# Block attention and a top-1 mixture of experts on one core: one cast and one subtraction for eight transposed blocks

## The chip, the cores and the metric

The kernel runs on one core of a Trainium2 chip. The metric is device time in microseconds, from the start of one execution to its end; less is better. Engines are named as the profile names them: PE (TensorE matmuls and transposes), PEld (its weight loads), DVE (VectorE), ACT (ScalarE), POOL (GpSimd) and SP, which only issues DMAs here.

## The reference, cut to what matters

Eight batches of eight heads, 576 positions, 64 numbers each. Attention is masked by blocks of 64: a query sees the keys of its own block and of all blocks before it. The outputs of all heads, 4608 rows of 512, then go through a mixture of eight experts, of which each row uses the one with the highest gate.

```
scores = (q @ k.T) / 8;  scores = -1e9 where block(query) < block(key)
attn   = exp(scores - rowmax);  attn /= sum(attn);  x = attn @ v
expert = argmax(x @ w_gate)
y      = relu(x @ w1[expert]) @ w2[expert] * gate(x) * sigmoid(x @ w_output_gate)
```

## The kernel before

Attention is worked on in 32 **pairs** of heads of one batch. A pair passes through the engines as a pipeline: `round_of(g)` writes the work of step g, four steps to a pair, and each step holds pieces of several pairs at different ages. Here a **period** is four steps (r = 0, 1, 2, 3), in which one pair enters and one leaves. The order on PE, ACT and DVE is the order in which the code is written; all three run it strictly in that order, and wait on semaphores of other engines. SP issues the loads (`fetch`, `fetch_v`) some steps ahead.

What a pair goes through, with the names that matter below:

- `turn` (r = 3): PE transposes eight 128 x 128 blocks of k and q, which lie in the tile `nat`, into one PSUM tile `ps_s`. Each number is kept as the sum of two 16-bit ones: ACT casts the transposed block to 16 bits (tile `tr0`, the high part), DVE subtracts it from the PSUM value (tile `tr1`, the low part). `turn_blocks` does this for four blocks at a time, and is called twice. The two tiles show as `tr` in the rows.
- The **ninth block** holds the 64 first positions of k and q, which fit in no block of 128. It is transposed in the next step r = 0, in `turn_max`, into the tile there.
- `max_tile` 0, 1 and 2 (r = 0, 1, 2): products of the high parts alone, of which DVE takes the row maxima (`nmx`). The maxima of the last query tile against the odd first 64 keys come apart, by `odds_rest` and `max_rest` (r = 3), in a corner of the tile of `prob_tile` 2; `nmr` holds them. Two small DVE operations (L199, L200) then finish the maxima as 16-bit numbers in `nmz`.
- `turn_max` (next r = 0): PE transposes `nmz`, and ACT copies the result to `qe`, by which the maxima are subtracted inside the products.
- `prob_tile` 3, 0, 1, 2 (r = 0, 1, 2, 3): the products in full, and their exponentials by ACT into `pcr` and `pc`.
- `lows` (POOL): the low part of each exponential, `lpc` and `lpcr`.
- `values` and `values_odd` (r = 2, 3): the products with v, into the PSUM tile `ps_v`; `norm` (DVE, r = 0) divides by the sums, and `turn_x` transposes the result for the gate.

`ps_s` has three buffers of two PSUM banks each, taken in turn; a period takes ten of them (and a few more where a batch ends). A tile that takes a buffer waits until the tile three places before it has been read by its last reader. Once in four periods a batch is complete, and `finish_batch` adds small pieces for its gates and for the table of rows.

After the attention come the experts (from about 600 us), whose products fill PE; no line of them is changed.

Of the kernel before, what the change touches and what calls it, by code (L numbers as in the profile page):

```python
# [8 lines left out]
F16 = mybir.dt.float16  # L9
BF16 = mybir.dt.bfloat16  # L10
F32 = mybir.dt.float32
I32 = mybir.dt.int32
U32 = mybir.dt.uint32
AF = mybir.ActivationFunctionType
ALU = mybir.AluOpType
AX = mybir.AxisListType
# [4 lines left out]
P = 128  # L21
# [5 lines left out]
def block_attention_top1_moe(  # L27
# [11 lines left out]
    nc = tc.nc  # L39
# [4 lines left out]
    NT = 5  # L44
# [4 lines left out]
    SCALE = D ** -0.5  # L49
# [19 lines left out]
    NPR = B * NP  # L69
# [5 lines left out]
    sb = tc.alloc_tile_pool(name="sb", bufs=2)  # L75
    small = tc.alloc_tile_pool(name="small", bufs=2)
# [5 lines left out]
    last_max, last_lo, last_exp = [None], [None], [None]  # L82
# [3 lines left out]
    def banks():  # L86
        return ps_s.tile([P, 2, 512], F32, name="ps_s")
# [4 lines left out]
    class Pair:  # L92
# [22 lines left out]
        def turn(self, ps=None):  # L115
            self.room()
            ps = banks() if ps is None else ps
            ps = ps.rearrange("p a (b n) -> p (a b) n", n=P)
            for w in range(2):
                self.turn_blocks(ps[:, 4 * w:4 * w + 4], 1 + 4 * w)  # L120

        def turn_blocks(self, ps, r, hi=None):
            n = ps.shape[1]
            for j in range(n):
                nc.tensor.transpose(ps[:, j], self.nat[:, r + j].rearrange("p h d -> p (h d)"), ident)  # L125
            th, tl = (self.tr[c][:, r:r + n] for c in range(2))
            (hi or nc.scalar.copy)(th, ps)  # L127
            nc.vector.tensor_tensor(tl, ps, th, ALU.subtract)  # L128

# [59 lines left out]
                    os[ab][:, c0:c0 + R0], self.asks(0, ab, n, n + 1)[:, 0], self.odd(0, ab, 0, R0), start=True, stop=True  # L189
                )  # L190

        def odds_rest(self, ps):
            self.odds([ps[:, ab] for ab in range(2)], 3, 256)

        def max_rest(self, ps):
            self.nmz = nmzs[self.p % 2]
            nmr = small.tile([P, 2], F32, name="nmr")
            last_max[0] = nc.vector.tensor_reduce(nmr, ps[:, :, 256:320], AX.X, ALU.max, negate=True)  # L198
            nc.vector.tensor_tensor(self.nmx[:, 3, :], self.nmx[:, 3, :], nmr, ALU.min)  # L199
            nc.vector.tensor_scalar(  # L200
                self.nmz.rearrange("p t (h c) -> p t h c", h=2)[:, :, :, 0], self.nmx, 1.0 / MS, None, ALU.mult
            )

        def turn_max(self):
            ps = banks()
            pm = ps[:, 0].bitcast(F16)
            for t in range(NT):
                nc.tensor.transpose(pm[:, P * t:P * t + P], self.nmz[:, t, :], ident16)
            self.qe = sb.tile([P, 640], F16, name="qe")
            nc.scalar.copy(self.qe, pm[:, 0:640])  # L210
            if self.p + 2 < NPR:
                pairs[self.p + 2].turn_blocks(ps[:, 1:2, 0:P], 0)

        def prob_tile(self, i, ps=None):
            names = ("pc13", "pc0", "pc2", "pcr")
            if i == 0:
                self.pt = [sb.tile([P, 2, n], F32, name=x) for x, n in zip(names, (512, 512, 256, S // 2))]
                self.pl = [sb.tile([P, 2, n], F16, name="l" + x) for j, (x, n) in enumerate(zip(names, (512, 512, 256, S // 2)))]
            ps = banks() if ps is None else ps
            qe = self.qe[:, 0:512].rearrange("p (n x) -> p n x", x=P)  # L220

            def products(os, ks, qs):
                half = [slice(64 * ab, 64 * ab + 64) for ab in range(2)]
                for j, (kc, qc) in enumerate(((0, 0), (1, 0), (0, 1), (2, 2))):
                    for ab in range(2):
                        nc.tensor.matmul(os[ab], ks(kc, ab), qs(qc, ab), start=j == 0, stop=j == 3)  # L226

            if i < 3:
                for c, c0 in (((1, 0), (3, 384)), ((0, 0),), ((2, 0),))[i]:
                    m = P * (4 - c)  # L230

                    def ks(kc, ab):
                        return self.keys(kc, ab, c, c + 1)[:, 0] if kc < 2 else kext[64 * ab:64 * ab + 64, c]

                    def qs(qc, ab):
                        return self.asks(qc, ab, c, 4) if qc < 2 else qe[64 * ab:64 * ab + 64, c:4]

                    products([ps[:, ab, c0:c0 + m].rearrange("p (n x) -> p n x", x=P) for ab in range(2)], ks, qs)
                ap = ps[:, :, 0:256] if i == 2 else ps
            else:  # L240
                flat = ps.rearrange("p a n -> p (a n)")

                def ks(kc, ab):
                    return self.odd(kc, ab, 0, R0) if kc < 2 else kext[64 * ab:64 * ab + 64, 4, 0:R0]

                def main(qc, ab):
                    return self.asks(qc, ab, 0, 4) if qc < 2 else qe[64 * ab:64 * ab + 64]

                def last(qc, ab):
                    return self.odd(qc, ab, R0, P) if qc < 2 else self.qe[64 * ab:64 * ab + 64, 576:640]  # L250

                halves = [flat[64 * ab:64 * ab + 64] for ab in range(2)]
                products([x[:, 0:512].rearrange("p (n x) -> p n x", x=P) for x in halves], ks, main)
                products([x[:, 512:S] for x in halves], ks, last)
                ap = flat[:, 0:S].rearrange("p (a n) -> p a n", a=2)
            self.ap = ap
            if i != 2:
                self.exps(i)

        def exps(self, i):  # L260
            last_exp[0] = nc.scalar.activation(self.pt[i], self.ap, AF.Exp, scale=SCALE)  # L261

        def lows(self, i):
            eng = nc.gpsimd if self.p < NPR - 4 else nc.vector
            eng.tensor_tensor(self.pl[i], self.pt[i], self.high(i), ALU.subtract)  # L265

        def high(self, j):
            return self.pt[j].bitcast(BF16)[:, :, 1::2]
# [53 lines left out]
        def turn_x(self):  # L322
            if self.hp == 0:
                xTs[self.b] = sb.tile([P, NP, S], F32, name="xT")
            pa = banks().rearrange("p a n -> p (a n)")
            for t in range(NT):
                nc.tensor.transpose(pa[:, P * t:P * t + P], self.xn[:, t], ident)
            xT = xTs[self.b]
            nc.scalar.copy(xT[:, self.hp, 0:512], pa[:, 0:512])
            nc.scalar.copy(xT[:, self.hp, 512:S], pa[:, 576:640])  # L330
            if self.hp == NP - 1:
                later.append(finish_batch(self.b, xT))

    xTs = {}

    with tc.high_priority(offset=3000):
        ident16 = const.tile([P, P], F16, name="ident16")
# [66 lines left out]
    def opening():  # L404


        x, y = Pair(0), Pair(1)
        x.fetch()
        y.fetch()
        rest = ps_v.tile([P, 2, 512], F32, name="ps_v")  # L410

        def turned(z):
            z.turn()
            z.turn_blocks(rest[:, z.p:z.p + 1, 0:P], 0, nc.vector.tensor_copy)

        turned(x)
        at(1, lambda: turned(y))
        return x, y

    with tc.manual_schedule(engines={mybir.EngineType.PE}), tc.high_priority(offset=2000):  # L420
        pairs = dict(enumerate(opening()))
# [49 lines left out]
    def pay_later():  # L471
        for g in list(later):
            if next(g, later) is later:
                later.remove(g)
# [534 lines left out]
    def round_of(g):  # L1009

        r = g % 4

        def do(back, name, *args):
            p, rr = divmod(g - back, 4)
            if 0 <= p < NPR:
                getattr(pairs[p], name)(*args)

        if r == 0:
            do(4, "turn_max")
            if g < 4 * NPR + 11:  # L1020
                do(16, "turn_x")
            do(12, "norm")
            do(0, "max_tile", 0)
            pay_later()
            do(8, "prob_tile", 3)
        elif r == 1:
            do(1, "max_tile", 1)
            do(5, "prob_tile", 0)
            do(9, "lows", 3)
            pay_later()  # L1030
            if g == 4 * NPR + 9:
                do(13, "turn_x")
        elif r == 2:
            do(6, "lows", 0)
            do(6, "prob_tile", 1)
            do(2, "max_tile", 2)
            pay_later()
            do(10, "values", 0)
            do(6, "lows", 1)
        else:  # L1040
            ps = banks() if g < 4 * NPR + 4 else None
            do(7, "prob_tile", 2, ps)
            do(3, "odds_rest", ps)
            do(3, "max_rest", ps)
            do(7, "exps", 2)
            do(-5, "turn")
            pay_later()
            do(11, "values_odd")
            do(11, "values", 1)
            do(7, "lows", 2)  # L1050
        for fn in events.get(g, ()):
            fn()
        pay_later()
# [124 lines left out]
```

## Time and profile before

| what | value |
| --- | --- |
| median of 3 runs (lowest, highest) | 980.36 us (976.35, 983.75) |
| the profiled execution: its time, its span | 985.71 us, 984.0 us |
| PE busy | 790.8 us, 80% of the span |
| PEld busy | 554.5 us, 56% |
| DVE busy | 608.7 us, 62% |
| ACT busy | 458.5 us, 47% |
| POOL busy | 395.9 us, 40% |

The busy shares are means over two stages. In the attention, which is about the first 560 us, PE is busy some seven tenths of the time and its granted clock lies between 0.7 and 0.9 of full speed; with the experts PE is busy nearly all the time at the full clock. The granted clock is a mean: the engine runs at 1.2 or at 2.4 GHz, and 0.5 in a stretch means that all of it was at 1.2. A row of a timeline tells the start, the duration and the work of an instruction (or of some alike), and in square brackets how long its engine had been idle before it and what ended that.

### The profile page before, as it was taken

The numbers are of one execution on the slowest core, as the hardware profiler recorded it, in microseconds if no ns is written. First come the engines' busy times: TensorE is split into PE (matmuls) and PEld (weight loads), VectorE is DVE, ScalarE is ACT, GpSimd is POOL, SyncE is SP. The second block draws the span as 40 slices with busy tenths as digits, with TensorE's granted clock in tenths as the row PEclk, the third lists the DMA queues.
The fourth block names the chain that finished last, engine by engine and source line by source line (L and its number), as shares of the span: only waits on it lengthen the run. The fifth ranks groups of instructions, "written<-read, shape, count | busy, mean of one in ns | idle before, by whom it ended". The sixth has DMA issues, their size and how long they took to land. (4 is left out here: it accounts for less than half of the span.)

```text
span 984.0 us, 23380 instructions
## 1 busy us (share of the span) xinstructions
PE 790.8 (80%) x9438; PEld 554.5 (56%) x9438; DVE 608.7 (62%) x962; ACT 458.5 (47%) x668; POOL 395.9 (40%) x348
## 2 busy tenths in 40 slices
PE   5676767767776767768676787799999999999995
PEld 3455545555554545555454574567766776667762
DVE  6555575656565665656668634778685968577560
ACT  2433434344343343343343521767665767475550
POOL 3544345455454363464425633634223233241101
PEclk9777797888798897888887799799999999999998
DMA  6342423224233323223125105897899998972330
GB/s 154 78 97 51 97 50 84 63 50 97 50 71 76 81 66 85 62 66 82 26 53 192 47 14 192 178 310 214 298 292 318 338 317 210 281 221 70 129 109 35
DMA packets 203748, 130.48 MB, mean 133 GB/s; under 512 B 157456, under 2 KB 175920, under 8 KB 203632
## 3 DMA queue, kind: packets, MB, share of 16 engines
q1 hardware_dynamic: 195584, 109.61, 40.8%
q0 software_dynamic: 8048, 19.29, 6.6%
q8 instruction: 76, 1.25, 0.6%
q14 instruction: 40, 0.33, 0.1%
HBM read 126.03 MB, written 19.34 MB: 148 GB/s over the span
## 5 line engine op out<-in xcount | busy, mean ns | idle before, releaser
L896 PEld LDWEIGHTS <-w1b 128*128 128x128 f16 (+1 forms) x2208 | 176.7, 98 | 25.2 <-issue 3.4
L896 PE MATMUL ps_s<-xt,w1b 128*128 128x256 f16 (+5 forms) x1920 | 175.8, 253 | 1.7 <-issue 1.3
L925 PE MATMUL ps_o<-w2b,hh 128*128 128x512 f16 (+1 forms) x560 | 168.6, 383 | 9.4 <-ACT hh L904 8.9
L125 PE MATMUL ps_s<-ident,nat 128*128 128x128 f32 x286 | 63.5, 341 | 135.5 <-DVE tr L128 104.9
L265 POOL TENSOR_TENSOR lpc<-pc 128x1024 f16<-128x1024 f32 (+1 forms) x84 | 133.8, 1612 | 54.5 <-ACT pc L261 54.1
L775 DVE TENSOR_TENSOR w2b<-w2f,w2b 128x1024 bf16<-128x1024 f32 x80 | 92.7, 1219 | 94.8 <-ACT w2b L773 82.5
L175 DVE TENSOR_REDUCE nmx<-ps_s 128x2 f32<-128x896 f32 (+4 forms) x160 | 120.1, 788 | 45.3 <-PE ps_s L188 24.4
L261 ACT ACTIVATE pc<-ps_s 128x1024 f32<-128x1024 f32 (+1 forms) x96 | 82.1, 880 | 119.4 <-DVE nmr L198 55.4
L128 DVE TENSOR_TENSOR tr<-ps_s,tr 128x512 f16<-128x512 f32 (+1 forms) x94 | 52.7, 561 | 134.7 <-ACT tr L127 132.7
L125 PEld LDWEIGHTS ps_s<-ident,nat 128*128 128x128 f32 x286 | 37.5, 163 | 154.4 <-DVE tr L128 113.1
L934 POOL DMA_INDIRECT out_dram<-ys,ids x38 | 49.4, 1300 | 153.2 <-ACT ys L933 90.9
L925 PE MATMUL ps_o<-w2b,hl 128*128 128x512 f16 x280 | 106.9, 382 | 0.0
L925 PEld LDWEIGHTS <-hh 128*128 128x128 f16 x560 | 54.8, 98 | 72.8 <-ACT hh L904 9.0
L226 PE MATMUL ps_s<-tr,tr 64*128 64x384 f16 (+5 forms) x768 | 95.6, 328 | 0.0
L127 ACT CAST tr<-ps_s 128x512 f16<-128x512 f32 (+1 forms) x94 | 45.3, 481 | 103.8 <-PE ps_s L125 103.8
L775 DVE TENSOR_TENSOR w1b<-w1f,w1b 128x1024 bf16<-128x1024 f32 x80 | 92.6, 1217 | 0.7 <-ACT w1b L773 0.6
L226 PEld LDWEIGHTS <-tr 64*128 64x128 f16 (+1 forms) x1152 | 56.2, 110 | 50.7 <-issue 31.7
L274 PE MATMUL ps_v<-vh,pc 128*128 128x65 f16 x640 | 82.8, 214 | 1.0 <-DVE xn L313 0.7
L265 POOL TENSOR_TENSOR lpcr<-pcr 128x576 f16<-128x576 f32 x28 | 32.1, 1146 | 127.6 <-ACT pcr L261 127.6
L275 PE MATMUL ps_v<-vl,pc 128*128 128x64 f16 x640 | 82.5, 212 | 0.5 <-issue 0.5
L276 PE MATMUL ps_v<-vh,lpc 128*128 128x65 f16 x640 | 82.4, 212 | 0.4 <-issue 0.4
L933 ACT ACTIVATE ys<-ps_o,ids 128x512 f32<-128x512 f32 (+1 forms) x38 | 26.1, 686 | 118.1 <-PE ps_o L925 100.0
(208 smaller groups left out, 1640.1 us busy)
## 6 DMA issues: line engine op xcount, KB each, us to landing
w1f<-in_moe_w_dram SPq DMA_DIRECT2D x80, 512.0 KB
w2f<-in_moe_w_dram SPq DMA_DIRECT2D x80, 512.0 KB
nat<-in_k_dram SPq DMA_DIRECT2D x64, 128.0 KB
nat<-in_q_dram SPq DMA_DIRECT2D x64, 128.0 KB
vn<-in_v_dram SPq DMA_DIRECT2D x64, 128.0 KB
x_d<-xn SPq DMA_DIRECT2D x32, 256.0 KB
hh<-in_moe_w_dram SPq DMA_DIRECT2D x4, 512.0 KB
hl<-in_moe_w_dram SPq DMA_DIRECT2D x4, 512.0 KB
```

The costliest lines, as they stand in the source:

```text
L125: nc.tensor.transpose(ps[:, j], self.nat[:, r + j].rearrange("p h d -> p (h d)"), ident)
L128: nc.vector.tensor_tensor(tl, ps, th, ALU.subtract)
L175: last_max[0] = nc.vector.tensor_reduce(self.nmx[:, t, :], ps[:, :, c0:c1], AX.X, ALU.max, negate=True)
L226: nc.tensor.matmul(os[ab], ks(kc, ab), qs(qc, ab), start=j == 0, stop=j == 3)
L261: last_exp[0] = nc.scalar.activation(self.pt[i], self.ap, AF.Exp, scale=SCALE)
L265: eng.tensor_tensor(self.pl[i], self.pt[i], self.high(i), ALU.subtract)
L274: nc.tensor.matmul(o, hi, self.vh[rows, j], start=first, stop=False)
L275: nc.tensor.matmul(o[:, 0:D], hi, self.vl[rows, j], start=False, stop=False)
L276: nc.tensor.matmul(o, lo, self.vh[rows, j], start=False, stop=last)
L775: eng.tensor_tensor(lo[at], src[at], hi[at], ALU.subtract)
L896: nc.tensor.matmul(ph[:, f4].rearrange("p (h n) -> p h n", n=w), wv[:, cc, f, :], xv[:, cc], start=(k == 0), stop=(k == 3 * KD - 1))
L925: nc.tensor.matmul(py, hv[:, f, h], wv[:, f, :], start=(k == 0), stop=(k == 3 * KF - 1))
```

## The change

- `turn` makes all eight transposes first, and then calls the new `halves` once: one cast and one subtraction of 128 x 1024 in the place of two of 128 x 512 each.
- The new `mixed` takes the place of `turn_max`, `odds_rest` and the first half of `max_rest`. In one PSUM tile at the start of r = 0 it has the transposes of the last pair's `nmz`, the ninth block of the pair to come, and the odd maxima's products of the pair now beginning. ACT copies `qe`; after `norm`, DVE takes the odd maxima and makes both halves of the ninth block (its cast was on ACT).
- The end of the maxima (the two small operations of `max_rest`) moves from r = 3 to r = 2, behind `max_tile` 2.
- `prob_tile` 2 takes its exponential at once, and shares its tile with nothing.
- `lows` 0 and 1 are cut into two instructions each, one for each head.

```diff
         def turn(self, ps=None):
...
-            for w in range(2):
-                self.turn_blocks(ps[:, 4 * w:4 * w + 4], 1 + 4 * w)
-
-        def turn_blocks(self, ps, r, hi=None):
-            n = ps.shape[1]
-            for j in range(n):
+            self.turn_blocks(ps, 1)
+            self.halves(ps, 1)
+
+        def turn_blocks(self, ps, r):
+            for j in range(ps.shape[1]):
                 nc.tensor.transpose(ps[:, j], self.nat[:, r + j].rearrange("p h d -> p (h d)"), ident)
-            th, tl = (self.tr[c][:, r:r + n] for c in range(2))
+
+        def halves(self, ps, r, hi=None):
+            th, tl = (self.tr[c][:, r:r + ps.shape[1]] for c in range(2))
             (hi or nc.scalar.copy)(th, ps)
             nc.vector.tensor_tensor(tl, ps, th, ALU.subtract)
...
         def lows(self, i):
             eng = nc.gpsimd if self.p < NPR - 4 else nc.vector
-            eng.tensor_tensor(self.pl[i], self.pt[i], self.high(i), ALU.subtract)
+            n = 2 if i < 2 else 1
+            for ab in range(n):
+                sl = slice(ab, ab + 1) if n == 2 else slice(0, 2)
+                eng.tensor_tensor(self.pl[i][:, sl], self.pt[i][:, sl], self.high(i)[:, sl], ALU.subtract)
...
+    def mixed(g):
+
+        p = g // 4
+        z, x, y = (pairs[j] if 0 <= j < NPR else None for j in (p - 1, p, p + 1))
+        y = y if p > 0 else None
+        ps = banks()
+        pm = ps[:, 0].bitcast(F16)
+        if z:
+            for t in range(NT):
+                nc.tensor.transpose(pm[:, P * t:P * t + P], z.nmz[:, t, :], ident16)
+        if y:
+            y.turn_blocks(ps[:, 1:2, 0:P], 0)
+        if x:
+            x.odds([ps[:, ab] for ab in range(2)], 3, 320)
+        if z:
+            z.qe = sb.tile([P, 640], F16, name="qe")
+            nc.scalar.copy(z.qe, pm[:, 0:640])
+        yield
+        if x:
+            x.nmr = small.tile([P, 2], F32, name="nmr")
+            last_max[0] = nc.vector.tensor_reduce(x.nmr, ps[:, :, 320:384], AX.X, ALU.max, negate=True)
+        if y:
+            y.halves(ps[:, 1:2, 0:P], 0, nc.vector.tensor_copy)
...
         if r == 0:
-            do(4, "turn_max")
+            parts = mixed(g) if g < 4 * NPR + 4 else iter(())
+            next(parts, None)
             if g < 4 * NPR + 11:
                 do(16, "turn_x")
             do(12, "norm")
+            next(parts, None)
             do(0, "max_tile", 0)
...
             do(2, "max_tile", 2)
+            do(2, "max_rest")
...
-            ps = banks() if g < 4 * NPR + 4 else None
-            do(7, "prob_tile", 2, ps)
-            do(3, "odds_rest", ps)
-            do(3, "max_rest", ps)
-            do(7, "exps", 2)
+            do(7, "prob_tile", 2)
             do(-5, "turn")
```

The order of PE in r = 3, around `turn`, first before and then changed. `nat` is the tile of loaded k and q, `ident` the identity matrix, and names in the brackets are semaphores: of DMA queues, of ACT (Activation) and of DVE.

```order
L188 LDWEIGHTS tr_2167
L188 MATMUL ps_s<-tr_2167 128x64
L125 MATMUL ps_s<-ident,nat 128x128 [waits DMAHW2_49,DMAHW1_49,Activation_49]
L125 MATMUL ps_s<-ident,nat 128x128 x3
L125 MATMUL ps_s<-ident,nat 128x128 [waits DMAHW7_49,DMAHW6_49,DVE_49]
L125 MATMUL ps_s<-ident,nat 128x128 x3
L274 LDWEIGHTS pcr
L274 MATMUL ps_v<-vh_101,pcr 128x65
```

```order
L212 LDWEIGHTS kext
L212 MATMUL ps_s<-qe,kext 128x256
L124 MATMUL ps_s<-ident,nat 128x128 [waits DMAHW7_49,DMAHW0_49,Activation_49]
L124 MATMUL ps_s<-ident,nat 128x128 x3
L124 MATMUL ps_s<-ident,nat 128x128 [waits DMAHW5_49,DMAHW4_49]
L124 MATMUL ps_s<-ident,nat 128x128 x3
L258 LDWEIGHTS pcr
L258 MATMUL ps_v<-vh_101,pcr 128x65
```

The fifth transpose waited for a DVE instruction, the subtraction of the first four; now it waits for its loads alone. The odd maxima's products (L188) are gone from here.

The order of PE at the start of r = 0, before and changed; `nmz` are the maxima, `xn` a finished pair's output, and `tr` in the last rows is the new pair's transposed tile.

```order
L208 MATMUL ps_s<-ident_77,nmz_96 128x128
L125 MATMUL ps_s<-ident,nat 128x128 [waits DMAHW3_49,DMAHW0_49,Activation_49]
L327 MATMUL ps_s<-ident,xn 128x128 [waits PE_49]
L327 MATMUL ps_s<-ident,xn 128x128 x4
L181 LDWEIGHTS tr_2428
L181 MATMUL ps_s<-tr_2428 128x384 [waits DVE_49]
```

```order
L327 MATMUL ps_s<-ident_77,nmz_96 128x128
L124 MATMUL ps_s<-ident,nat 128x128 [waits DMAHW6_49,DMAHW3_49]
L189 LDWEIGHTS tr_2424
L189 MATMUL ps_s<-tr_2424 128x64
L189 LDWEIGHTS tr_2424
L189 MATMUL ps_s<-tr_2424 128x64
L311 MATMUL ps_s<-ident,xn 128x128 [waits Activation_49]
L311 MATMUL ps_s<-ident,xn 128x128 x4
L182 LDWEIGHTS tr_2424
L182 MATMUL ps_s<-tr_2424 128x384 [waits DVE_49]
```

The ninth block no longer waits for ACT's copy of `qe`, and the odd maxima's products stand between it and `turn_x`.

The order of DVE over a period, from `norm` on, before and changed; `sm` and `xn` are `norm`, and `tr` the low parts.

```order
L311 TENSOR_SCALAR sm<-ps_v 128x10
L312 RECIPROCAL sm<-sm 128x10
L313 TENSOR_TENSOR xn<-ps_v,sm 128x2x5x64
L175 TENSOR_REDUCE nmx<-ps_s 128x2 x5
L198 TENSOR_REDUCE nmr<-ps_s 128x2
L199 TENSOR_TENSOR nmx<-nmx,nmr 128x2
L200 TENSOR_SCALAR nmz_96<-nmx 128x10
L128 TENSOR_TENSOR tr_3765<-ps_s,tr_3764 128x512 x2
L128 TENSOR_TENSOR tr_3765<-ps_s,tr_3764 128x128
```

```order
L295 TENSOR_SCALAR sm<-ps_v 128x10
L296 RECIPROCAL sm<-sm 128x10
L297 TENSOR_TENSOR xn<-ps_v,sm 128x2x5x64
L338 TENSOR_REDUCE nmr<-ps_s 128x2
L128 CAST tr_3760<-ps_s 128x128
L129 TENSOR_TENSOR tr_3761<-ps_s,tr_3760 128x128
L176 TENSOR_REDUCE nmx<-ps_s 128x2 x5
L195 TENSOR_TENSOR nmx<-nmx,nmr 128x2
L196 TENSOR_SCALAR nmz_97<-nmx 128x10
L129 TENSOR_TENSOR tr_4332<-ps_s,tr_4331 128x1024
```

The odd maxima and the ninth block now stand behind `norm` and ahead of the five reductions, and one subtraction stands where there were two.

## Rows read from the trace of the kernel before

**Rows 1.** Waits of the whole execution: engine, line, releaser; total us, times, longest.

```profile
PE ps_s L125 <- DVE tr L128: 104.9, 33, 3.8
ACT pc L261 <- DVE nmr L198: 55.4, 17, 9.6
PE ps_s L125 <- ACT qe L210: 26.2, 30, 1.6
```

**Rows 2.** Busy time by stretch: PE, PEld, DVE, ACT, POOL, clock, DMA share, GB/s.

```profile
287.93:302.93 15.00, 10.42 (x183) 7.77 (x183) 9.47 (x14) 6.48 (x11) 10.08 (x8) 0.93 0.34 82
302.93:319.58 16.65, 12.07 (x183) 8.55 (x183) 9.56 (x14) 6.48 (x11) 7.17 (x5) 0.81 0.30 72
319.58:339.08 19.50, 14.91 (x210) 10.18 (x210) 11.88 (x26) 7.56 (x15) 7.21 (x5) 0.78 0.26 62
339.08:356.18 17.10, 11.20 (x183) 8.26 (x183) 9.92 (x22) 6.48 (x12) 9.30 (x8) 0.90 0.30 71
```

**Rows 3.** Timeline of PE from 300 to 335 us.

```profile
303.68 0.48 PE L125 MATMUL ps_s<-ident,nat 128*128 128x128 f32 x1 [0.84 <-ACT qe L210]
...
308.65 0.34 PE L226 MATMUL ps_s<-tr 64*128 64x384 f16 x2 [0.41 <-ACT pcr L261]
...
310.38 0.40 PE L181 MATMUL ps_s<-tr 64*128 64x512 f16 x2
...
310.74 0.20 PE L274 MATMUL ps_v<-vh,pc 128*128 128x65 f16 x1
...
311.75 0.28 PE L226 MATMUL ps_s<-tr 64*128 64x256 f16 x2
...
312.32 0.66 PE L125 MATMUL ps_s<-ident,nat 128*128 128x128 f32 x4
316.31 0.66 PE L125 MATMUL ps_s<-ident,nat 128*128 128x128 f32 x4 [3.33 <-DVE tr L128]
```

**Rows 4.** Busy time by stretch, columns as in the second group.

```profile
304.00:307.40 3.40, 3.40 (x22) 1.87 (x22) 2.60 (x6) 0.96 (x3) 0.00 (x0) 0.50 0.68 152
...
313.00:316.30 3.30, 0.00 (x0) 0.00 (x0) 3.22 (x3) 0.89 (x2) 2.64 (x2) 1.00 0.00 0
```

**Rows 5.** Timeline of PE from 356 to 372 us.

```profile
357.08 0.71 PE L327 MATMUL ps_s<-ident,xn 128*128 128x128 f32 x5
357.73 0.34 PE L181 MATMUL ps_s<-tr 64*128 64x384 f16 x2
...
358.08 0.40 PE L226 MATMUL ps_s<-tr 64*64 64x512 f16 x2
...
359.19 0.28 PE L181 MATMUL ps_s<-tr 64*128 64x256 f16 x2
```

**Rows 6.** Groups by form: count, busy us, mean ns of one, idle before.

```profile
L265 POOL TENSOR_TENSOR lpc<-pc 128x1024 f16<-128x1024 f32 x56 | 105.3, 1897 | 44.0 <-ACT pc L261 43.9
...
L261 ACT ACTIVATE pc<-ps_s 128x1024 f32<-128x1024 f32 x64 | 63.0, 1022 | 42.6 <-PE ps_s L226 34.7 <-POOL lpcr L265 6.2 <-PE ps_s L493 1.7
...
L905 DVE SCALAR_TENSOR_TENSOR hl<-ps_s,hh 128x1024 bf16<-128x1024 f32 x30 | 36.6, 1220 | 6.5 <-ACT hh L904 6.4
...
L265 POOL TENSOR_TENSOR lpc<-pc 128x512 f16<-128x512 f32 x28 | 29.1, 1041 | 10.4 <-ACT pc L261 10.3
...
L128 DVE TENSOR_TENSOR tr<-ps_s,tr 128x128 f16<-128x128 f32 x30 | 8.7, 291 | 79.5 <-ACT tr L127 79.5
```

**Rows 7.** Timeline of DVE from 300 to 335 us.

```profile
304.70 0.16 DVE L311 TENSOR_SCALAR sm<-ps_v 128x10 f32<-128x10 f32 x1
...
305.88 1.28 DVE L175 TENSOR_REDUCE nmx<-ps_s 128x2 f32<-128x896 f32 x2
...
312.44 0.29 DVE L198 TENSOR_REDUCE nmr<-ps_s 128x2 f32<-128x128 f32 x1 [0.37 <-PE ps_s L188]
```

**Rows 8.** All executions of two DVE lines: count, duration ns min/median/max.

```profile
L199 DVE TENSOR_TENSOR nmx<-nmx,nmr x32: 160/1139/1899, 17.7 to 541.6; 128x2 f32<-128x2 f32 x32
...
L200 DVE TENSOR_SCALAR nmz<-nmx x32: 189/592/1845, 17.9 to 541.8; 128x10 f16<-128x10 f32 x32
```

More of the change, by code (lines that the diff above doesn't have):

```diff
@@ L190, in odds, with max_rest @@
                 )
-        def odds_rest(self, ps):
-            self.odds([ps[:, ab] for ab in range(2)], 3, 256)
-        def max_rest(self, ps):
+        def max_rest(self):
             self.nmz = nmzs[self.p % 2]
-            nmr = small.tile([P, 2], F32, name="nmr")
-            last_max[0] = nc.vector.tensor_reduce(nmr, ps[:, :, 256:320], AX.X, ALU.max, negate=True)
-            nc.vector.tensor_tensor(self.nmx[:, 3, :], self.nmx[:, 3, :], nmr, ALU.min)
+            nc.vector.tensor_tensor(self.nmx[:, 3, :], self.nmx[:, 3, :], self.nmr, ALU.min)
             nc.vector.tensor_scalar(
@@ L202, in max_rest, with prob_tile @@
             )
[L204 to L214, printed above, removed]
+        def prob_tile(self, i):
             names = ("pc13", "pc0", "pc2", "pcr")
@@ L218, in prob_tile @@
                 self.pl = [sb.tile([P, 2, n], F16, name="l" + x) for j, (x, n) in enumerate(zip(names, (512, 512, 256, S // 2)))]
-            ps = banks() if ps is None else ps
+            ps = banks()
             qe = self.qe[:, 0:512].rearrange("p (n x) -> p n x", x=P)
@@ L255, in prob_tile @@
                 ap = flat[:, 0:S].rearrange("p (a n) -> p a n", a=2)
[L256 to L261, printed above, removed]
+            last_exp[0] = nc.scalar.activation(self.pt[i], ap, AF.Exp, scale=SCALE)
         def lows(self, i):
             eng = nc.gpsimd if self.p < NPR - 4 else nc.vector
-            eng.tensor_tensor(self.pl[i], self.pt[i], self.high(i), ALU.subtract)
+            n = 2 if i < 2 else 1
+            for ab in range(n):
+                sl = slice(ab, ab + 1) if n == 2 else slice(0, 2)
+                eng.tensor_tensor(self.pl[i][:, sl], self.pt[i][:, sl], self.high(i)[:, sl], ALU.subtract)
         def high(self, j):
@@ L332, in turn_x @@
                 later.append(finish_batch(self.b, xT))
+    def mixed(g):
+        p = g // 4
+        z, x, y = (pairs[j] if 0 <= j < NPR else None for j in (p - 1, p, p + 1))
+        y = y if p > 0 else None
+        ps = banks()
+        pm = ps[:, 0].bitcast(F16)
[15 more added lines that the diff above has]
+            y.halves(ps[:, 1:2, 0:P], 0, nc.vector.tensor_copy)
     xTs = {}
@@ L413, in turned @@
             z.turn()
-            z.turn_blocks(rest[:, z.p:z.p + 1, 0:P], 0, nc.vector.tensor_copy)
+            z.turn_blocks(rest[:, z.p:z.p + 1, 0:P], 0)
+            z.halves(rest[:, z.p:z.p + 1, 0:P], 0, nc.vector.tensor_copy)
         turned(x)
```

## The prediction

> **What bounds the kernel now.** I read the list of waits first. PE, which has most to do of all engines, stands still for 104.9 us in 33 waits in front of a transpose of `nat` (L125) until DVE has finished a subtraction, and for 26.2 us in 30 more until ACT has copied `qe` [rows 1]. No other wait of PE in the attention is near these. The timeline of PE shows the place: four transposes at 312.32, 3.33 us of nothing, four more at 316.31 [rows 3]. The second four write another half of the same tile, but the program lets them wait until DVE has subtracted the first four. The 0.84 us ahead of the ninth block, at 303.68, has the same form: the tile's other half is being read by ACT [rows 3].
>
> Next, the table of four periods (a batch's work falls into the last two). They take 15.00, 16.65, 19.50 and 17.10 us, 17.06 in the mean, and each holds one wait of either kind, 4.17 us together [rows 2, 3]. PE is busy for 10.42 us of the shortest. DVE is busy for 9.47 to 11.88, POOL for 7.17 to 10.08, ACT for 6.48 to 7.56 [rows 2]. So no engine fills a period, and the reader should see a loop with a hole in it rather than a full engine; the question is which loop is next.
>
> The clock belongs to this. The first two periods hold the same instructions (183 on PE, 14 on DVE, 11 on ACT; POOL differs by three), and the one at 0.81 takes 1.65 us longer than the one at 0.93 [rows 2]. In the hole the granted clock still reads 1.00; some microseconds after an earlier hole of this kind it reads 0.50, with PE busy throughout the stretch [rows 4].
>
> **The change, part by part.** *Eight transposes in a row.* The order shows that the fifth waits for its loads alone. The 104.9 us go, unless the loads are late; in the hole at 313 the DMA share is 0.00, so nothing was being loaded that could be [rows 4].
>
> *The ninth block ahead of the `qe` copy.* The 26.2 us go as well: 131.1 us of PE's idle time in all.
>
> *What is late next.* The tiles go round three buffers, so each one waits for a reader of an earlier one. By the order, `prob_tile` 3 in r = 0 now needs the buffer of `mixed`, whose last reader on DVE stands behind the subtraction of `turn` and behind `norm`. I add up that chain from the end of the eight transposes: ACT's cast of 1024, 1.02 us by the exponential of that size; the subtraction of 1024, 1.22 us by the row of L905, which also takes 1024 numbers out of PSUM into 16 bits [rows 6]; `norm`, 304.70 to 305.88, 1.18 us; the odd maxima, 0.29 [rows 7]; cast and subtraction of the ninth block, 0.29 each at most, by the row of its subtraction [rows 6]. That is 4.29 us, and with an allowance of 0.1 for each of four handovers 4.7.
>
> Meanwhile PE has the products with v (two sets; one lasts from 310.74 to 311.75, so 2.02) [rows 3], the transposes of the maxima with the ninth block and the odd products (no row at the full clock; between nothing and the 0.65 of the five larger transposes, I take 0.5), `turn_x` 0.65 (357.08 to 357.73) and `max_tile` 0 0.35 (to 358.08) [rows 5]: 3.5 us at the full clock. So a **new wait** of 4.7 - 3.5 = 1.2 us stands in front of `prob_tile` 3 when PE runs at 2.4 GHz, and none at 1.2 GHz, where the 3.5 become up to 7.
>
> The rest of PE's round is `prob_tile` 3 1.11 (358.08 to 359.19) [rows 5], `max_tile` 1 as 2 0.36, `prob_tile` 0 and 1 1.73 (308.65 to 310.38), `max_tile` 2 0.36, products with v 1.01, `prob_tile` 2 0.57 (311.75 to 312.32) and eight transposes, twice 0.66 [rows 3]: 6.46 us. PE alone therefore needs 3.5 + 6.46 = 10.0 us, near the 10.42 of its row, and the loop 6.46 + 4.7 = 11.2. Taking the two holes out of the shortest period gives 15.00 - 4.17 = 10.83, so the two ways agree within half a microsecond.
>
> *The clock.* With the holes gone it may stay up. Between the alike periods that is worth up to 1.65 us; but a period at the full clock has the new wait of 1.2. I take the two as equal, and put the difference into the range.
>
> *The odd maxima earlier.* Their exponential (`prob_tile` 2) no longer waits for `nmr`, 55.4 us of ACT's idle time [rows 1]. ACT is idle for more than half of a period, so I count nothing for it but the earlier start of the cast, which is in the chain above. The rule of the Trainium skill that speaks against the shared tile (PSUM — Partial Sum Buffer, section on bank collisions) is that two engines must be kept apart on one bank even when both only read; the 55.4 us agree with it, since ACT and DVE both read that tile. By it the odd maxima wait for the `qe` copy in the new tile; if the cover by `norm` were gone, that would be at most 1.02 us a pair (the longer exponential), 31 us in 30 pairs, and without the rule nothing.
>
> *The two small operations of the maxima* (L199, L200) take 0.16 and 0.19 us when alone and 1.14 and 0.59 in the median [rows 8]. They now stand behind `max_tile` 2. From the end of that tile to the end of the new cast PE and ACT need 1.01 + 0.57 + 1.32 + 1.02 = 3.9 us; DVE needs 1.22 for the maxima (1024 numbers out of PSUM, as in the row of L905) and 0.35 to 1.73 for the two, at most 2.95 by the medians. Covered; uncovered it would cost the 1.4 by which they are stretched.
>
> *POOL.* A low part of 1024 takes 1897 ns, one of 512 takes 1041, so two cuts cost 2 x 185 ns a pair [rows 6]. Unless POOL fills the period this is hidden behind it: 8.4 us busy in the mean of the four, 8.8 then, against some 12.9.
>
> **The sum.** 131.1 us go. Three of the 33 waits, 9.5 us at the mean of 3.2, lie in the opening or outside the 30 steady rounds (pairs 2 to 31), where the first loads hide them: 121.6 remain, 4.05 for each of 30 pairs. The new wait and the clock cancel. The profiled execution took 985.71 us, with 1.7 of it outside its span of 984.0; it becomes 864. On the median of 980.36 that is **858 us**, and I predict this.
>
> **The rivals.** *The port (900 us).* L199 varies from 160 to 1899 ns, and a POOL operation of 1024 lasts 1897 [rows 6, 8]: the small operation seems to wait for the whole of POOL's. If in the shorter period these waits fall on the chain ahead of the subtraction, 1.4 us a pair come back, 42 in 30 pairs. For it: DVE is in the new loop, and a batch adds up to 2.4 us to it [rows 2]. Against it: the cover above, and POOL's pieces, which are half as long now. The Trainium skill states such a rule (SBUF — State Buffer, section on the two separate sides): VectorE and GpSimd share a port pair that one holds for a whole instruction. The rows agree. By the rule each of the two waits would end within 1.04 us, 2.1 a pair at most.
>
> *No new wait (818 us).* If the chain is shorter than I think and the clock stays up, PE sets the period: 10.0, and 0.41 for the one small wait left at 308.65 [rows 3], and the batch's share. That share is (19.50 + 17.10 - 15.00 - 16.65) / 4 = 1.24 us. 17.06 - 11.65 = 5.4 a pair, 162 in 30. For it: PE's row; against it: the order, which has the wait.
>
> *The hole stays (954 us).* The second four wait for the loads of q instead, and only the 26.2 us go. Against it stands the DMA share of 0.00.
>
> *Slower (1087 us).* The clock stays at 1.2 GHz: PE's 10.42 x 0.93 = 9.7 us of work at the full clock become 19.4, with the batch's share 20.6, 3.6 more than now, 107 us in 30 pairs. It decides from a mean clock of 9.7 / (17.06 - 1.24) = 0.61 downwards. The four periods show 0.78 to 0.93 with the holes in them, so I give it little.
>
> **How the numbers follow.** The forecast, with 840 to 885 around it, has 0.68; the port 0.17, no new wait 0.10, the hole that stays 0.02, slower 0.03. The range for eight in ten runs from 826 to 902: it takes in the port's case and half of the way to the PE-bound one, and leaves out the ends. One per cent is about what a measurement of this kernel can tell from no change: 0.95 for faster, 0.02 for within it, 0.03 for slower.
>
> **What would show it.** Right: no wait for DVE in front of the transposes of `nat`, none for ACT in front of the ninth block, periods of 12.5 to 13.2 us in the mean, and a wait for DVE's ninth subtraction in front of the first product of `prob_tile` 3. The granted clock of the attention lies above 0.85. The stage of the experts lasts as long as now and starts some 120 us earlier. Wrong: a hole of over 2 us in another place of the period, or a DVE whose busy share of a period passes 0.9.

## The result, and the profile after

The changed kernel takes 853.76 us (median of 4 runs, 851.51 to 854.52) where the kernel before takes 979.67 on the same chip: a ratio of 0.871, with a 95% interval from 0.867 to 0.875. The forecast was 858 in a range from 826 to 902. The profiled execution has a span of 852.1 us where it was 984.0.

The page's first part, which answers to the table ahead of the prediction:

```profile
PE 745.4 (87%) x9438; PEld 525.9 (62%) x9438; DVE 628.6 (74%) x968; ACT 448.3 (53%) x606; POOL 396.9 (47%) x404
```

From this one row the gain can be split. PE stood still for 984.0 - 790.8 = 193.2 us of the span, and now does for 852.1 - 745.4 = 106.7: 86.5 us of idle time are gone. Its busy time fell by 45.4 us, though it runs the same 9438 matmuls. That fits the granted clock, whose mean rose (first before, then changed):

```profile
core 0: 984.0 us, clock 0.897
core 0: 852.1 us, clock 0.943
```

The two parts make up the 131.9 us between the spans.

PE's waits in the changed kernel (engine, line, releaser; total us, times, longest):

```profile
PE ps_s L327 <- DVE nmz L196: 20.8, 7, 3.4
PE ps_v L259 <- POOL vl L150: 12.5, 7, 3.6
PE ps_s L182 <- ACT xT L314: 11.1, 6, 2.0
PE ps_s L212 <- ACT xT L314: 7.5, 20, 0.5
...
PE ps_s L124 <- DMA nat<-in_k_dram: 4.1, 1, 4.1
...
PE ps_s L212 <- DVE tr L129: 3.5, 7, 1.1
```

The waits of [rows 1] in front of the transposes of `nat` are gone, both of them; what is left there is the first load. New are those for `nmz`, for POOL's low part of v, and for `xT`.

The table of stretches of the changed kernel (PE, PEld, DVE, ACT, POOL, clock, DMA share, GB/s); the first four rows are four periods that answer to [rows 2], the fifth is five periods before the first batch is complete, the last is 21 of the periods with batches:

```profile
210.85:225.94 15.09, 9.81 (x184) 7.21 (x184) 13.86 (x15) 6.11 (x9) 13.64 (x13) 0.99 0.34 80
225.94:236.82 10.88, 10.69 (x185) 7.80 (x186) 8.76 (x15) 6.17 (x10) 5.83 (x6) 0.85 0.46 111
236.82:250.86 14.04, 12.19 (x215) 8.64 (x215) 12.43 (x26) 7.23 (x12) 9.07 (x9) 1.00 0.36 86
250.86:262.93 12.07, 10.35 (x179) 7.43 (x179) 8.45 (x23) 6.05 (x11) 5.46 (x6) 0.86 0.43 101
...
28.26:77.74 49.48, 45.98 (x907) 34.34 (x903) 41.28 (x68) 29.26 (x42) 36.88 (x36) 1.00 0.54 128
...
104.88:381.00 276.12, 227.19 (x3979) 164.05 (x3979) 235.83 (x398) 134.08 (x204) 181.26 (x173) 0.93 0.37 88
```

Without batches a period takes 9.9 us at the full clock, and PE is busy for 93% of it: there PE itself is the bound. With batches it takes 13.15 us in the mean. The same two groups of pairs in the kernel before:

```profile
31.79:115.17 83.38, 61.33 (x905) 43.38 (x905) 46.51 (x68) 31.02 (x52) 37.10 (x26) 0.77 0.30 70
...
151.53:508.02 356.49, 254.83 (x3978) 182.74 (x3978) 213.18 (x397) 141.43 (x246) 174.46 (x130) 0.85 0.28 68
```

That is 16.68 and 16.98 us a period: those without a batch gained 6.8 us each, those with batches 3.8. In the changed kernel the first of the four rows is the odd one: 15.09 us with hardly more instructions than the next, POOL busy for 13.64 of them and DVE for 13.86.

### The profile page after: what moved, and what is told of

It is laid out like the page before. It is cut to its first block, busy times and chain, and to the rows that moved or that the text cites. A ratio compares the mean times of both kernels' runs of the same rounds, so it can differ in the third digit from the quotient of the medians.

```text
span 852.1 us, 23354 instructions
## 1 busy us (share of the span) xinstructions
PE 745.4 (87%) x9438; PEld 525.9 (62%) x9438; DVE 628.6 (74%) x968; ACT 448.3 (53%) x606; POOL 396.9 (47%) x404
## 5 line engine op out<-in xcount | busy, mean ns | idle before, releaser
L249 POOL TENSOR_TENSOR lpc<-pc 128x512 f16<-128x512 f32 x140 | 141.7, 1043 | 33.5 <-ACT pc L242 33.2
L943 POOL DMA_INDIRECT out_dram<-ys,ids x38 | 46.6, 1228 | 160.8 <-ACT ys L942 92.2
L212 PE MATMUL ps_s<-tr 64*128 64x256 f16 (+5 forms) x384 | 65.8, 331 | 23.1 <-ACT xT L314 7.5
L782 ACT CAST w1b<-w1f 128x1024 f16<-128x1024 f32 x80 | 78.3, 1045 | 3.4 <-DMA w1f<-in_moe_w_dram 3.2
L782 ACT CAST w2b<-w2f 128x1024 f16<-128x1024 f32 x80 | 77.8, 1043 | 1.1 <-DMA w2f<-in_moe_w_dram 1.1
L259 PE MATMUL ps_v<-vl,pc 128*128 128x64 f16 x640 | 66.4, 195 | 12.5 <-POOL vl L150 12.5
L754 POOL DMA_INDIRECT xg<-x_d,ids x38 | 50.2, 1322 | 42.2 <-DMA ids<-tab_d 13.8
L260 PEld LDWEIGHTS <-lpc 128*128 128x128 f16 x640 | 59.6, 99 | 13.1 <-issue 13.1
L258 PE MATMUL ps_v<-vh,pc 128*128 128x65 f16 x640 | 67.7, 198 | 0.0
```

Source lines behind the costliest of these rows:

```text
L249: eng.tensor_tensor(self.pl[i][:, sl], self.pt[i][:, sl], self.high(i)[:, sl], ALU.subtract)
L258: nc.tensor.matmul(o, hi, self.vh[rows, j], start=first, stop=False)
L259: nc.tensor.matmul(o[:, 0:D], hi, self.vl[rows, j], start=False, stop=False)
L260: nc.tensor.matmul(o, lo, self.vh[rows, j], start=False, stop=last)
L754: nc.gpsimd.indirect_dma_start(out=xg[i % NXG][0:width[i], h], out_offset=None, in_=x_d[0:nx, :], in_offset=IOA(ap=ids[i][0:width[i], h, 0 ...
L782: nc.scalar.copy(hi, src)
```

## The experiments

All ran beside the kernel before. In four of them (one cast alone, all but the one cast, the low parts whole, the end of the maxima without the port) the kernel before took 979.59 us, nearly as above, so times are compared too. In the other six it took 983 to 985 us, so there ratios are compared: 0.871 is the changed kernel. Differences of ratios are given in points, hundredths of the time before.

**One cast alone.** The kernel before with the first item of the change.

```diff
-            for w in range(2):
-                self.turn_blocks(ps[:, 4 * w:4 * w + 4], 1 + 4 * w)
+            self.turn_blocks(ps, 1)
```

> The kernel before, with one part of the change: all eight transposes, then one cast and one subtraction of 128 x 1024. The ninth block, the odd maxima and the low parts stay as they were. Theory (the hole in front of the second four transposes carried the gain): 95 to 110 us less than before, 870 to 885 us, and the list of waits has none for a DVE subtraction in front of a transpose of nat beyond some 5 us. Rival (the gain needs the odd maxima out of the tile of the last exponentials, since their 55 us of ACT idle time delay the cast and with it the whole loop): under 70 us less, above 910 us, the exponential of 128 x 512 still late behind nmr.

It took 886.16 us, ratio 0.905 (0.902 to 0.908), 93 us less; the theory's range began at 95. Three of its waits:

```profile
ACT pc L260 <- DVE nmr L197: 56.5, 23, 10.2
...
PE ps_s L124 <- ACT qe L209: 43.0, 30, 3.6
...
PE ps_s L207 <- DVE nmz L199: 26.2, 22, 3.1
```

The exponential is as late behind `nmr` as in [rows 1] (56.5 us against 55.4), and the gain is there all the same, so the rival falls. Of the 104.9 us that are gone, 17 come back in front of the ninth block (26.2 to 43.0) and nearly 25 in front of the maxima's transposes (1.6 to 26.2).

**All but the one cast.** The changed kernel with `turn` in two passes.

```diff
-            self.turn_blocks(ps, 1)
-            self.halves(ps, 1)
+            for w in range(2):
+                self.turn_blocks(ps[:, 4 * w:4 * w + 4], 1 + 4 * w)
+                self.halves(ps[:, 4 * w:4 * w + 4], 1 + 4 * w)
```

> The changed kernel with the transposes in two passes again (four, cast, subtraction, four, cast, subtraction); all other parts of the change stay. Theory (the hole is the matter): it comes back at some 2 to 3 us a pair, shorter than before since the small operations of the maxima no longer stand ahead of the first subtraction: 60 to 100 us more than the changed kernel, 915 to 955 us. Rival (the odd maxima and the ninth block carry the gain): less than 30 us more, under 885 us.

909.11 us, ratio 0.929 (0.926 to 0.932): 55 us more than the changed kernel, just short of the theory's 60 and well beyond the rival's 30. The hole is back, shorter (2.4 us a pair, not 3.2):

```profile
PE ps_s L125 <- DVE tr L130: 78.3, 32, 4.7
```

So the one cast saves 9.5% alone and the rest 7.1% alone, but both together 12.9%: this fits one loop, in which each hides part of the other.

**The ninth block, added to the one cast.** It is transposed ahead of the copy of `qe`, its halves made on DVE.

```diff
...
+                nc.tensor.transpose(ps[:, 1, 0:P], y.nat[:, 0].rearrange("p h d -> p (h d)"), ident)
             self.qe = sb.tile([P, 640], F16, name="qe")
             nc.scalar.copy(self.qe, pm[:, 0:640])
...
-                pairs[self.p + 2].turn_blocks(ps[:, 1:2, 0:P], 0)
...
+                nc.vector.tensor_copy(th, ps[:, 1:2, 0:P])
+                nc.vector.tensor_tensor(tl, ps[:, 1:2, 0:P], th, ALU.subtract)
```

> The first experiment's kernel (one cast and one subtraction, all else as before) and the ninth block transposed ahead of the copy of qe, with both its halves on DVE; the odd maxima stay in the tile of the last exponentials, at the end of the period. Theory (the waits are one loop, and each part takes its own wait away): the 43.0 us that PE waited for the copy of qe go, some of it turns up in front of nmz, and the time is 15 to 35 us below the first experiment's 886, 851 to 871 us. Rival (without the earlier odd maxima the wait moves whole to nmz): within 10 us of 886, with PE's waits for nmz above 55 us.

863.25 us, ratio 0.877 (0.873 to 0.881): 2.8 points less than the one cast alone, as the theory has it. The wait for `nmz` even fell from 26.2 to 13.5 us:

```profile
PE ps_s L207 <- DVE nmz L199: 13.5, 18, 2.6
```

What the earlier odd maxima, the earlier end of the maxima and the cut low parts add on top is then 0.6 points, with intervals that overlap: no gain of theirs is shown.

**The ninth block, taken out of the change.** It stands behind the copy of `qe` again, and its cast is on ACT again.

```diff
-        if y:
-            y.turn_blocks(ps[:, 1:2, 0:P], 0)
         if x:
             x.odds([ps[:, ab] for ab in range(2)], 3, 320)
         if z:
             z.qe = sb.tile([P, 640], F16, name="qe")
             nc.scalar.copy(z.qe, pm[:, 0:640])
+        if y:
+            y.turn_blocks(ps[:, 1:2, 0:P], 0)
+            y.halves(ps[:, 1:2, 0:P], 0)
...
-        if y:
-            y.halves(ps[:, 1:2, 0:P], 0, nc.vector.tensor_copy)
```

> The changed kernel with the ninth block behind the copy of qe again and its cast on ACT; the odd maxima stay early. Theory (each part takes its own wait away): PE waits for the copy of qe about 0.8 to 1.4 us in each of 30 pairs, and the time is 15 to 40 us above the changed kernel's 854, 869 to 894 us. Rival (that wait is covered by others once the odd maxima are early): within 8 us of 854.

878.30 us, ratio 0.889 (0.885 to 0.894), 1.8 points more than the changed kernel. Against the one cast alone (0.905) the other parts give 1.6 points here. The wait is the one expected, 1.35 us a pair:

```profile
PE ps_s L124 <- ACT qe L332: 40.5, 30, 2.7
```

**The low parts whole.** POOL's low parts of 1024 in one instruction again (`n = 1` in `lows`).

> The changed kernel with the low parts of 1024 in one POOL instruction each again. Theory A (a small DVE operation waits until POOL's whole run of queued instructions is over, so that the length of one does not matter): within 8 us of the changed kernel, 846 to 860 us, and the operation that takes the minimum (L195 there) is still found with 5 us and more. Theory B (it waits for the one instruction under way, 1.04 us when cut and 1.90 when whole): the wait grows by some 0.4 to 0.9 us a pair, 10 to 25 us more, 864 to 880 us, and none is longer than 2.1 us.

853.67 us, ratio 0.872 (0.868 to 0.877): no difference. The minimum's line, all executions (ns, min/median/max), reaches 7.9 us with the low parts whole (first row) and 8.1 with them cut (second row, the changed kernel):

```profile
L195 DVE TENSOR_TENSOR nmx<-nmx,nmr x32: 160/702/7878, 17.3 to 411.3; 128x2 f32<-128x2 f32 x32
L195 DVE TENSOR_TENSOR nmx<-nmx,nmr x32: 161/828/8119, 17.2 to 411.3; 128x2 f32<-128x2 f32 x32
```

So cutting `lows` is worth nothing measurable, and the longest waits aren't set by the length of one POOL instruction.

**The end of the maxima without the port.** The odd maxima go to a column of `nmx`, the minimum is a reduction over two columns of it, the scaling is ACT's.

```diff
...
-            nc.vector.tensor_tensor(self.nmx[:, 3, :], self.nmx[:, 3, :], self.nmr, ALU.min)
-            nc.vector.tensor_scalar(
-                self.nmz.rearrange("p t (h c) -> p t h c", h=2)[:, :, :, 0], self.nmx, 1.0 / MS, None, ALU.mult
+            nc.vector.tensor_reduce(self.nmx[:, 3, :], self.nmx[:, 5:7, :].rearrange("p t h -> p h t"), AX.X, ALU.min)
+            nc.scalar.activation(
+                self.nmz.rearrange("p t (h c) -> p t h c", h=2)[:, :, :, 0], self.nmx[:, 0:NT, :], AF.Copy, scale=1.0 / MS
             )
...
```

> The changed kernel, with the end of the maxima done in another way: the minimum of the last tile's two maxima is a DVE reduction over two columns of one tile instead of an operation with two SBUF inputs, and the scaling into nmz is ACT's. Theory (those two operations stand still while POOL works and hold DVE's queue, which is what stretches the periods with a batch's work from about 10 to about 13 us): both take some 0.2 us, and the time falls by 20 to 45 us, to 810 to 834 us. Rival (POOL itself is late in those periods, for it also writes the table, and PE waits for POOL's low part of v in its place): under 10 us less, above 844 us, with the waits of PE for vl growing past 30 us.

826.91 us, ratio 0.844 (0.841 to 0.847): 27 us less than the changed kernel, the fastest of all. The two operations by form (count, busy us, mean ns), first here:

```profile
L192 DVE TENSOR_REDUCE nmx<-nmx 128x2 f32<-128x4 f32 x32 | 5.0, 158 | 1.1
...
L193 ACT ACTIVATE nmz<-nmx 128x10 f16<-128x10 f32 x32 | 8.0, 249 | 37.1 <-DVE nmx L192 37.1
```

and in the changed kernel:

```profile
L195 DVE TENSOR_TENSOR nmx<-nmx,nmr 128x2 f32<-128x2 f32 x32 | 59.0, 1844 | 1.1
...
L196 DVE TENSOR_SCALAR nmz<-nmx 128x10 f16<-128x10 f32 x32 | 22.3, 697 | 1.1
```

So 5.0 and 8.0 us stand in the place of 59.0 and 22.3. PE's wait for the low part of v stays at 12.2 us (12.5 in the changed kernel), where the rival had it grow past 30: the rival falls, though POOL is still late at times. Both operations changed at once, so what each of them gave is not shown. The stretches of this kernel that answer to the fifth and the last row of the table above:

```profile
27.87:79.52 51.65, 47.38 (x899) 34.87 (x899) 33.63 (x63) 29.90 (x48) 37.57 (x36) 0.97 0.51 121
105.46:358.80 253.34, 218.94 (x3983) 159.62 (x3983) 181.18 (x378) 136.69 (x225) 181.46 (x173) 0.96 0.40 96
```

A period with batches falls from 13.15 to 12.06 us, and one without takes 10.33 (9.9 in the changed kernel): the gain lies in the periods with batches.

**The minimum twice.** The changed kernel with its line issued twice.

> The changed kernel with the minimum of the maxima (two SBUF inputs) issued twice in a row; the second changes nothing in the values. Theory A (the operation stands until POOL has no instruction queued, so that the second one finds POOL idle or near it): the second takes 0.16 us in most pairs, where the first took over 2 us, and the time grows by at most 10 us, to 854 to 864 us. Theory B (each such operation loses to one POOL instruction): the second takes about as long as the first in the mean, 0.6 us and more, and the time grows by 15 to 35 us.

858.17 us, ratio 0.868 (0.862 to 0.874), no difference, where theory B had 15 us and more. The timeline of DVE has both kinds side by side:

```profile
130.65 0.87 DVE L195 TENSOR_TENSOR nmx<-nmx,nmr 128x2 f32<-128x2 f32 x1
131.55 0.96 DVE L196 TENSOR_TENSOR nmx<-nmx,nmr 128x2 f32<-128x2 f32 x1
...
223.42 7.27 DVE L195 TENSOR_TENSOR nmx<-nmx,nmr 128x2 f32<-128x2 f32 x1
230.73 0.16 DVE L196 TENSOR_TENSOR nmx<-nmx,nmr 128x2 f32<-128x2 f32 x1
```

In most periods each of the two loses to one POOL instruction, as theory B has it; four times the first stands for over 7 us and the second takes 0.16, as theory A has it. Neither holds alone.

**The table's writes spread.** Two more empty steps behind each of POOL's five writes of the table, for the first five batches; once in the changed kernel, once in the one without the port.

```diff
             yield
+            if b < B - 3:
+                yield
+                yield
```

> The changed kernel with POOL's writes of the table spread in the same way for the first five batches. Theory (the long waits of the minimum, 7 to 8 us once in four pairs, come where POOL is behind, because these writes stand among its low parts): in the first five batches the 7 us waits go and none is over 2.5 us; those of the batches that are not spread stay; the ratio falls from 0.871 to between 0.852 and 0.865. Rival (they come from the order alone, whatever POOL has queued): they stay, and the ratio is within 0.004 of 0.871.

849.95 us, ratio 0.863 (0.857 to 0.868), lower than 0.871 with intervals that just overlap. Of the changed kernel's five waits of over 7 us, three stayed (6.2 to 7.3 us) and two went. The timelines of POOL and of DVE, where one went and where one stayed:

```profile
217.35 1.15 POOL L249 TENSOR_TENSOR lpcr<-pcr 128x576 f16<-128x576 f32 x1
218.82 5.03 POOL L249 TENSOR_TENSOR lpc<-pc 128x512 f16<-128x512 f32 x5 [0.31 <-ACT pc L242]
```

```profile
220.31 0.56 DVE L195 TENSOR_TENSOR nmx<-nmx,nmr 128x2 f32<-128x2 f32 x1
```

```profile
164.14 1.16 POOL L249 TENSOR_TENSOR lpcr<-pcr 128x576 f16<-128x576 f32 x1
165.24 5.02 POOL L249 TENSOR_TENSOR lpc<-pc 128x512 f16<-128x512 f32 x5
170.23 1.27 POOL L150 TENSOR_TENSOR vl<-vn,vh 128x576 f16<-128x576 f32 x1
```

```profile
164.26 7.25 DVE L195 TENSOR_TENSOR nmx<-nmx,nmr 128x2 f32<-128x2 f32 x1
```

The long wait went where POOL caught up far enough to wait for ACT itself (0.31 us) ahead of its run, and stayed where it went from one instruction to the next; DVE's 7.25 us end with POOL's last one, at 171.5. That the backlog matters is supported; the theory's full form (none over 2.5 us) isn't. The pause itself is not what let DVE in: its minimum began at 220.31, 1.5 us behind the pause, inside the five low parts, and ended with the second of them. Where the wait stayed, it began at 164.26, ahead of these five. So where in POOL's run the operation begins is a rival to the backlog that no run here takes apart.

The same spreading in the kernel without the port:

> The kernel without the two port-bound operations, and POOL's writes of the table (five of about 1 us for each batch) spread over three times as many steps for the first five batches of eight. Theory (POOL's backlog after these writes is what is left of the long periods): PE's waits for the low part of v (12 us in 8 waits before) fall to under 6, and the ratio to the kernel before falls from 0.844 to 0.832 to 0.841. Rival (a batch's other work, on PE, DVE and ACT, makes these periods long): within 0.004 of 0.844.

834.35 us, ratio 0.849 (0.844 to 0.854). The waits for the low part of v fell from 12.2 to 3.7 us, as the theory has it:

```profile
PE ps_v L256 <- POOL vl L150: 3.7, 3, 1.3
```

Yet the ratio is not below 0.844, so the theory's gain falls. The 0.849 lies just beyond the rival's 0.004; that a batch's other work sets these periods fits, but is argued and not shown.

**A batch's exponential a step later**, in the kernel without the port: `zs` is issued behind the next `yield` of `finish_batch`.

> The kernel without the two port-bound operations (827 us), and one exponential of a batch's gates (zs) issued one step later on ACT, where its DVE operand should be ready. In the changed kernel's trace ACT stood 1.7 us in front of it, with the copies of qe and xT queued behind, and PE waited 2.0 us for xT in each batch. Theory: those waits of PE (12 us in the experiment before) go, 4 to 14 us less, 813 to 823 us. Rival (another wait of the batch is as long): within 4 us of 827.

836.21 us, ratio 0.848 (0.845 to 0.852), where the kernel without the port has 0.844: no gain. The wait at `max_tile` 0 fell from 12.1 to 4.7 us, and came back at `prob_tile` 3, whose waits were 8.6 and 3.5 us:

```profile
PE ps_s L209 <- ACT xT L311: 17.9, 20, 2.9
PE ps_s L209 <- DVE tr L129: 11.4, 7, 1.6
```

## Why the prediction was right

*The waits that go* (131.1 us). Right: none of the two is left, and the two experiments on each part show that each carries its own.

*The first loads hide three of them.* These three were put at nothing. The first copy of `qe` comes 1.7 us earlier (20.42 to 18.75), the second 3.5; from the second-last copy to the end of the span it is 458.7 us, and was 462.4. So the opening and the end gave 7.2 us of the 131.9, and the 29 periods between gave the rest: the gain lies in the attention, as forecast. (The forecast's last step, worked out, gives 859 rather than 858.)

*The period.* 12.5 to 13.2 us were forecast in the mean; the 29 periods (from 28.26 to 393.42) have 12.59, where they had 16.89 before (31.79 to 521.62): 4.30 a pair less, and 4.05 were put down. But this mean hides two kinds: 6.8 less without a batch, 3.8 less with one.

*The new wait and the clock cancel.* Right in the total: 131.1 - 86.5 = 44.6 us of idle time came back, and the clock gave 45.4. That they come out so near is luck, for the place was wrong, and this is the step that failed. I let `prob_tile` 3 wait for the ninth block's subtraction in every pair, 1.2 us at the full clock, some 36 us in 30 pairs. In a period without batches, PE and DVE (timelines, changed kernel):

```profile
68.93 0.41 PE L212 MATMUL ps_s<-tr 64*64 64x512 f16 x2 [0.43 <-ACT xT L314]
```

```profile
69.24 0.29 DVE L129 TENSOR_TENSOR tr<-ps_s,tr 128x128 f16<-128x128 f32 x1
```

`prob_tile` 3 starts before that subtraction does, after 0.43 us for `xT`: by this wait it has `turn_x`'s buffer here, not `mixed`'s. So the three buffers of `ps_s` don't always go round in turn, as the text ahead of the prediction has it. The forecast wait is found in some periods with a batch's work, but short:

```profile
147.01 0.51 PE L212 MATMUL ps_s<-tr 64*64 64x512 f16 x2 [0.40 <-DVE tr L129]
```

It makes 3.5 us in seven waits, in the list above. With the clock up and only such small waits, the periods without a batch are the rival "no new wait": 9.9 us, where its sum had 10.0 and 0.41.

*The batch's share* was put at 1.24 us a pair from [rows 2]; it is 13.15 - 9.9 = 3.2. Part of the reason is the rival that I had called the port. The small operations were said to be covered. In the period of 15.09 us, on DVE, POOL and PE (timelines, changed kernel):

```profile
217.55 7.30 DVE L195 TENSOR_TENSOR nmx<-nmx,nmr 128x2 f32<-128x2 f32 x1
224.88 0.19 DVE L196 TENSOR_SCALAR nmz<-nmx 128x10 f16<-128x10 f32 x1
```

```profile
217.47 1.14 POOL L249 TENSOR_TENSOR lpcr<-pcr 128x576 f16<-128x576 f32 x1
218.57 5.02 POOL L249 TENSOR_TENSOR lpc<-pc 128x512 f16<-128x512 f32 x5
223.56 1.27 POOL L150 TENSOR_TENSOR vl<-vn,vh 128x576 f16<-128x576 f32 x1
```

```profile
225.13 0.45 PE L327 MATMUL ps_s<-ident,nmz 128*128 128x128 f16 x5 [3.38 <-DVE nmz L196]
```

An operation with two SBUF inputs of two numbers each held DVE for 7.30 us, through seven instructions of POOL, with the subtraction of `turn`, `norm` and PE's next transposes behind. The rule of the Trainium skill that I weighed (SBUF — State Buffer, section on the two separate sides) has one engine hold the shared ports for a whole instruction, so that such an operation would wait for one. One low part takes 1.04 us here; the trace has waits for one instruction and waits for seven, and the measurement decides. Taking the two operations off the port gave 27 us back, and a period with batches fell from 13.15 to 12.06 us. So 1.1 of these 3.2 us are shown to be theirs, about a third; what makes the rest is open.

Both signs of being wrong that I had named appeared, in five periods of this kind: a hole of 3.4 us in another place, in front of the transposes of `nmz`, and in the period above a DVE that is busy for 13.86 of 15.09 us, 0.92.

So the number was right through two errors that offset each other: periods without batches came out shorter than forecast, those with batches longer. That the holes go, and what they were worth, was foreseen; that the two errors balance is luck. The cut of `lows`, put at nothing, measures at nothing.

## What to carry to other kernels

Where an engine waits inside one step for a reader of its own tile, write all of the tile first and read it in one go. The list of waits prices this only roughly: here 131.1 us of waits went, 86.5 us of idle time stayed away, and PE's busy time fell by 45.4 us with the higher clock. Then look for the next wait in every kind of period, the rare ones too: buffers need not go round in turn, and one period's order is not all of them. A tiny VectorE operation with two SBUF inputs beside a busy GpSimd deserves a look, whatever its size: rewriting two that take 0.16 and 0.19 us alone (as a reduction over two columns, and on ScalarE) gave 27 us here.

## What the runs showed of the hardware that was not expected

The minimum with two SBUF inputs takes 0.16 us alone. In the changed kernel it lasted 0.5 to 0.9 us where it began in the second or third of five low parts in a row on POOL, and ended with the one under way. Where it began ahead of these five, while POOL worked through a backlog, it stood for 7.2 to 8.1 us, until the five and the low part of v behind them were done; this happened five times. Three more, which began beside a write of the table, took 2.15 to 2.35 us. As a reduction over two columns it took 0.158 us in the mean, beside a POOL as busy. What decides between the short and the long wait stays open.
